# Two batches of a fused attention and feed-forward kernel: loads through one casting queue, and transposes moved from DMA to TensorE

## The chip, the cores and the metric

The kernel runs on one core of one Trainium2 chip. The metric is the device time of one execution in microseconds. The median of three runs before the change is 457.38 us.

## The reference

```python
def _attn_ref(q, k, v):                  # (8 batches, 12 heads, 448, 64) each
    S = q.shape[2]
    scale = 1.0 / np.sqrt(q.shape[-1])
    scores = scale * np.matmul(q, k.transpose(0, 1, 3, 2))
    attn = np.maximum(scores, 0.0) ** 2 / S
    return np.matmul(attn, v)

def _moe_ref(x, w_in, w_out):            # x (3584, 768), w_in (768, 2048), w_out (2048, 768)
    h = x @ w_in
    g = h * (1.0 / (1.0 + np.exp(-1.702 * h)))
    return g @ w_out
```

x is the attention's output with the heads side by side: row (batch, position), column (head, 64).

## The kernel before

**Units and slots.** The attention is cut into 24 units, three for each of 8 batches, with four heads each. The four heads are two pairs (s) of two (a). A unit's q, k and v lie with 128 partitions = (s, 64 positions) and, in each, 2 heads a by 7 x 64 values. A unit has seven slots j, one per seventh of its keys. A slot is `scores` (L124): four matmuls of 64x64 weights and 448 columns into a PSUM tile of the pool `ps_s`, which has two; `relu2` (L138): a relu on ScalarE (ACT), or on VectorE (DVE) in slot 3 of the first six units, and a square on VectorE; and `av_mm` (L149): the weighted sum, four matmuls, accumulated over the seven slots. `xt_evac` (L164) copies a finished unit into the activations `xt` of its group of tokens.

**Visits.** `visit(n)` (L184) issues the scores of the next n slots (two as a rule), then the weighted sums of the slots of the visit before, then the relus and squares of the new ones. All engines work in program order; nothing is reordered (L281).

**Products.** The tokens are cut into groups of 384 and 512 rows in turn. `m1(g, f)` (L204) is one of 16 column tiles of the first product: six matmuls on weights `win`, an activation on ScalarE and a scaling on GpSimd (POOL). `m2(g, m, h)` (L224) is the second product, 16 matmuls on `wout`. Both take PSUM from the pool `ps_m` (two buffers).

**How q and k come in.** `load_qk` (L73) loads f32 from SyncE's (SP's) queue. `cast` (L92) makes f16 on VectorE or GpSimd. `trans` (L103) turns it with DMA transposes, issued from SP, so that the 64 values of two heads lie on 128 partitions. Only unit 0 is turned by `trans_pe` (L111): seven transposes of 128 columns on TensorE (PE) into a tile of `ps_s`, copied out by ScalarE and VectorE. v is loaded and cast by one DMA on GpSimd's queue (L83), as are the weights: `w1(i)` (L246) brings a quarter of w_in in four DMAs, `w2(h, i)` (L253) a quarter of w_out in one. `sp_gate` (L259) and `pool_gate` (L262) hold a queue until something has landed.

**Order at the start (L281 to L339).** Units 0 to 2 are loaded from SP, v and the quarters of w_in come between from GpSimd, units 3 and 4 behind a gate. The slots of units 0 to 2 (batch 0) run alone (L299, L317). Then the 16 column tiles of the first group's first product alternate with the slots of units 3 to 5 (L322 to L337); in between, units 4 and 5 are cast and transposed and w_out is loaded. At L355 a gate waits for a quarter of w_out, the loads of units 6 and 7 are issued, and the first group's second product begins (L357). From there on products and visits alternate by a table of costs (L366 to L405), and each later unit is loaded and cast some units ahead.

The places that the prediction speaks of are the first score (L131), the first product proper (L212), the first second product (L230) and the first score of unit 6.

Of the kernel before, what the change touches and what calls it, by code (L numbers as in the profile page):

```python
# [15 lines left out]
def kernel(  # L16
# [9 lines left out]
    nc = tc.nc  # L26
# [19 lines left out]

    cst = ctx.enter_context(tc.tile_pool(name="cst", bufs=1))
    stp = ctx.enter_context(tc.tile_pool(name="stp", bufs=3))
    c16 = ctx.enter_context(tc.tile_pool(name="c16", bufs=2))
    v16p = ctx.enter_context(tc.tile_pool(name="v16p", bufs=5))  # L50
    qkT = ctx.enter_context(tc.tile_pool(name="qkT", bufs=3))
    rlp = ctx.enter_context(tc.tile_pool(name="rlp", bufs=3))
# [8 lines left out]

    ident = cst.tile([128, 128], F16, name="ident")
    gate = cst.tile([1, 64], F16, name="gate")
    gate2 = cst.tile([1, 1], F32, name="gate2")
    warm = cst.tile([1, 1], F32, name="warm")
    win = [cst.tile([128, 2, NP, WQ * 128], F16, name=f"win{i}") for i in range(NF // WQ)]
    wout = [[cst.tile([128, WO, NOUT], F16, name=f"wout{h}_{i}") for i in range(NF // WO)]
            for h in range(2)]


    units = {}

    def load_qk(u):  # L73
        b, pr = divmod(u, NP)
        st = units.setdefault(u, {})
        for n, t in (("k", k), ("q", q)):
            x = stp.tile([128, 2, S], F32, name=f"{n}st", tag=f"{n}st")
            nc.sync.dma_start(
                out=x,
                in_=t[b, 4 * pr:4 * pr + 4].rearrange("(a s) (p j) d -> (s p) a (j d)", a=2, j=J))  # L80
            st[n] = x

    def load_v(u):  # L83
        b, pr = divmod(u, NP)
        st = units.setdefault(u, {})
        x = v16p.tile([128, 2, S], F16, name="v16", tag="v16")
        nc.gpsimd.dma_start(  # L87
            out=x,
            in_=v[b, 4 * pr:4 * pr + 4].rearrange("(a s) (p j) d -> (s p) a (j d)", a=2, j=J))
        st["v16"] = x  # L90

    def cast(u, n, eng):  # L92
        st = units[u]
        c = c16.tile([128, J, 2, D], F16, name=f"{n}16", tag=f"{n}16")
        o = c.rearrange("p j a d -> p a j d")
        i = st[n].rearrange("p a (j d) -> p a j d", d=D)
        if eng is nc.scalar:
            eng.activation(out=o, in_=i, func=AF.Copy)
        else:
            eng.tensor_copy(out=o, in_=i)  # L100
        st[n + "16"] = c

    def trans(u):  # L103
        st = units[u]
        for n in ("k", "q"):
            t = qkT.tile([128, J, 128], F16, name=f"{n}T", tag=f"{n}T")
            nc.sync.dma_start_transpose(  # L107
                out=t[:, :, :], in_=st[n + "16"].rearrange("p j a d -> p (j a d)"))
            st[n + "T"] = t

    def trans_pe(u, n, cut):  # L111
        st = units[u]
        ps = ps_s.tile([128, 2, 1024], F16, name="tr", tag="sc")
        for j in range(J):
            nc.tensor.matmul(  # L115
                out=ps[:, 0, j * 128:(j + 1) * 128],
                lhsT=st[n + "16"][:, j, :, :], rhs=ident[:, :], is_transpose=True)
        t = qkT.tile([128, J, 128], F16, name=f"{n}T", tag=f"{n}T")
        nc.scalar.activation(out=t[:, 0:cut, :], in_=ps[:, 0, 0:cut * 128], func=AF.Copy)
        if cut < J:  # L120
# [17 lines left out]
    def relu2(u, j, sc):  # L138
        rl = rlp.tile([128, 2, S], F16, name="rl", tag="rl")
        at = atp.tile([128, 2, S], F16, name="at", tag="at")  # L140
        if u < 2 * NP and j == 3:
            nc.vector.tensor_scalar(out=rl, in0=sc[:, :, 0:S], scalar1=0.0, scalar2=None,  # L142
                                    op0=ALU.max)
        else:
            nc.scalar.activation(out=rl, in_=sc[:, :, 0:S], func=AF.Relu)  # L145
        nc.vector.tensor_tensor(out=at, in0=rl, in1=rl, op=ALU.mult)  # L146
        return at
# [16 lines left out]
    def xt_evac(u):  # L164
        b, pr = divmod(u, NP)
        av = units[u]["av"]
        lo = b * J
        while lo < (b + 1) * J:
            g = max(i for i in range(NG) if gcum[i] <= lo)
            hi = min((b + 1) * J, gcum[g + 1])  # L170
            if g not in xts:
                xts[g] = xtp.tile([128, 2, NP, 512], F16, name="xt", tag="xt")
            nc.vector.tensor_copy(  # L173
                out=xts[g][:, :, pr, 64 * (lo - gcum[g]):64 * (hi - gcum[g])],
                in_=av[:, :, 64 * (lo - b * J):64 * (hi - b * J)])
            lo = hi
        units[u] = None
# [26 lines left out]
    def m1(g, f):  # L204
        n = 64 * gblk[g]
        if f == 0:
            gts[g] = gtp.tile([128, NF, 512], F16, name="gt", tag="gt")
        ht = ps_m.tile([128, 512], F32, name="ht", tag="mm")
        w = win[f // WQ]
        fo = (f % WQ) * 128  # L210
        for kk in range(NK):
            nc.tensor.matmul(  # L212
                out=ht[:, 0:n], lhsT=w[:, kk // NP, kk % NP, fo:fo + 128],
                rhs=xts[g][:, kk // NP, kk % NP, 0:n],
                start=(kk == 0), stop=(kk == NK - 1))
        gf = gfp.tile([128, 512], F32, name="gf", tag="gf")
        nc.scalar.activation(out=gf[:, 0:n], in_=ht[:, 0:n],  # L217
                             func=AF.Gelu_apprx_sigmoid, scale=1.0 / SC)
        nc.gpsimd.tensor_scalar(out=gts[g][:, f, 0:n], in0=gf[:, 0:n],  # L219
                                scalar1=SC, scalar2=1.0, op0=ALU.mult, op1=ALU.mult)  # L220
# [20 lines left out]
                nc.sync.dma_start(out=out[r0:r0 + 63 * J + 1:J, :],  # L241
                                  in_=ot[64 * i:64 * i + 64, :])

    w_rows = moe_w_in.rearrange("(i a s d) f -> a d s i f", a=2, s=2, d=D)

    def w1(i):  # L246
        for a in range(2):
            for s in range(2):
                nc.gpsimd.dma_start(  # L249
                    out=win[i][64 * a:64 * a + 64, s, :, :],  # L250
                    in_=w_rows[a, :, s, :, i * WQ * 128:(i + 1) * WQ * 128])

    def w2(h, i):  # L253
        nc.gpsimd.dma_start(  # L254
# [26 lines left out]
    with tc.manual_schedule():  # L281
        nc.vector.memset(warm, 0.0)
        nc.scalar.activation(out=warm, in_=warm, func=AF.Gelu_apprx_sigmoid)
        make_identity(nc, ident)


        load_qk(0)
        load_qk(1)
        load_qk(2)
        load_v(0)  # L290
        cast(0, "k", nc.vector)
        trans_pe(0, "k", J)
        cast(0, "q", nc.vector)
        trans_pe(0, "q", 4)
        pool_gate(units[1]["k"][0:1, 0, 0:1])
        load_v(1)
        w1(0)
        cast(1, "k", nc.vector)
        visit(2)  # L299
        cast(1, "q", nc.vector)  # L300
        trans(1)
        cast(2, "k", nc.gpsimd)
        cast(2, "q", nc.gpsimd)
        trans(2)
        load_v(2)
        w1(1)
        sp_gate(win[0][64:65, 1, 0, 0:64])
        load_qk(3)
        load_v(3)
        w1(2)  # L310
        cast(3, "k", nc.gpsimd)
        cast(3, "q", nc.gpsimd)
        trans(3)
        load_qk(4)
        load_v(4)
        w1(3)
        while pos[0] < NP * J:  # L317
            visit(min(2, NP * J - pos[0]))
        visit(0)


        for f in range(NF):  # L322
            m1(0, f)
            if f >= 1 and (f % 4 != 3 or f == 15):
                visit(min(2, 2 * NP * J - pos[0]))
            if f == 2:
                cast(4, "k", nc.vector)
                cast(4, "q", nc.gpsimd)
                trans(4)
                load_qk(5)  # L330
                load_v(5)
            if f in (4, 5, 6, 7):
                w2((f - 4) // 2, f % 2)
            if f == 7:
                cast(5, "k", nc.vector)
                cast(5, "q", nc.gpsimd)
                trans(5)  # L337
# [98 lines left out]
```

## Time and profile before

| | us |
|---|---|
| median of 3 runs (455.9 to 1011.11) | 457.38 |
| the profiled execution | 456.6 |
| its span, first to last instruction | 454.8 |
| TensorE busy | 394.2 (87%) |
| ScalarE busy | 206.5 (45%) |
| VectorE busy | 193.9 (43%) |
| GpSimd busy | 132.4 (29%) |

Durations come from the profiled execution; its span is 1.8 us shorter than its time. Of the three runs one took 1011.11 us, the others 455.9 and 457.38. The profile names engines PE, PEld (weight loads of PE), DVE, ACT, POOL and SP; a matmul's duration runs from its start to its modelled end, so that overlapped matmuls add up to more than the time that they take together.

### The profile page before, as it was taken

How to read it: one execution, taken by the hardware profiler on the slowest of the kernel's cores; microseconds unless marked ns; L12 is line 12 of the kernel's file. 1: busy time of each engine (PE TensorE's matmuls, PEld its weight loads, DVE VectorE, ACT ScalarE, POOL GpSimd, SP SyncE). 2: the span in 40 equal slices, each digit the busy share in tenths (PEclk: the TensorE clock that was granted, in tenths of full speed). 3: DMA queues.
4: the chain of work that ended last, by engine and by line, in shares of the span. 5: the costliest groups of instructions: out<-in, count | busy, mean ns of one | idle time of the engine just before them, and what ended most of it. 6: DMA issues, size and time to landing. Idle time of an engine off the chain costs nothing.

```text
span 454.8 us, 7541 instructions
## 1 busy us (share of the span) xinstructions
PE 394.2 (87%) x3022; PEld 196.1 (43%) x3022; DVE 193.9 (43%) x292; ACT 206.5 (45%) x294; POOL 132.4 (29%) x203
## 2 busy tenths in 40 slices
PE   3255816299999999999999999999998999999995
PEld 1122303045443455544444555544444555555563
DVE  2555423343265565533644456455425643100121
ACT  4244424251577655536564555356555554222100
POOL 3714322213443422313323323313322311222200
PEclk9995767789999999999999999999999999999999
DMA  8999696954879772771853648745513311111132
GB/s 258 142 197 164 145 149 141 198 215 62 182 177 169 179 184 59 160 183 69 180 124 71 161 93 173 175 122 102 136 36 76 75 36 37 35 36 31 27 83 71
DMA packets 74340, 55.89 MB, mean 123 GB/s; under 512 B 45120, under 2 KB 70720, under 8 KB 74304
## 3 DMA queue, kind: packets, MB, share of 16 engines
q1 hardware_dynamic: 60288, 43.59, 39.5%
q0 software_dynamic: 14016, 11.80, 18.6%
q8 instruction: 24, 0.39, 0.4%
q14 instruction: 12, 0.10, 0.1%
HBM read 45.61 MB, written 11.01 MB: 124 GB/s over the span
## 4 chain that ended last, share of the span: by engine, by line
PE 74%; DMA 10%; DVE 5%; ACT 4%; issue 3%; POOL 2%; SPq 2%; ACTq 0%
PE op L230 31%; PE ht L212 30%; DMA qT<-q 8%; PE sc L131 7%; PE av L156 6%; ACT rl L145 3%; DVE xt L173 2%; DVE at L146 2%; DMA kst<-in_k_dram 2%; SPq L107 1%; DVE rl L142 1%; DVE k L100 1%; ACT gf L217 1%; POOL win L249 0%; DVE osb L235 0%
## 5 line engine op out<-in xcount | busy, mean ns | idle before, releaser
L145 ACT ACTIVATE rl<-sc 128x896 f16<-128x896 f32 x162 | 140.2, 918 | 92.2 <-PE sc L131 88.9
L212 PE MATMUL ht<-xt,win 128*128 128x384 f16 (+1 forms) x768 | 163.7, 359 | 4.4 <-DVE xt L173 4.4
L146 DVE TENSOR_TENSOR at<-rl 128x896 f16<-128x896 f16 x168 | 115.2, 703 | 113.1 <-ACT rl L145 112.9
L219 POOL TENSOR_SCALAR gt<-gf 128x384 f16<-128x384 f32 (+1 forms) x128 | 76.1, 595 | 270.1 <-ACT gf L217 268.8
L230 PE MATMUL op<-wout,gt 128*128 128x384 f16 x896 | 153.3, 326 | 0.0
L217 ACT ACTIVATE gf<-ht 128x384 f32<-128x384 f32 (+1 forms) x128 | 69.8, 545 | 123.3 <-PE ht L212 103.3
L230 PEld LDWEIGHTS <-gt 128*128 128x128 f16 x896 | 86.4, 98 | 62.9 <-issue 5.4
L212 PEld LDWEIGHTS <-win 128*128 128x128 f16 x768 | 71.4, 99 | 86.7 <-issue 29.8
L131 PE MATMUL sc<-qT,kT 64*64 64x448 f16 x672 | 55.9, 389 | 41.6 <-DMA qT<-q 32.4
L235 DVE TENSOR_SCALAR osb<-op 128x384 f32<-128x384 f32 x56 | 31.1, 556 | 114.8 <-PE op L230 114.8
L156 PE MATMUL av<-at,v 64*64 64x448 f16 x672 | 53.6, 379 | 4.0 <-DVE at L146 3.5
L131 PEld LDWEIGHTS <-kT 64*64 64x64 f16 x672 | 16.2, 109 | 76.2 <-issue 75.4
L173 DVE CAST xt<-av 128x768 f16<-128x768 f32 (+2 forms) x36 | 26.9, 774 | 21.7 <-PE av L156 21.4
L156 PEld LDWEIGHTS <-v 64*64 64x64 f16 x672 | 22.9, 112 | 21.5 <-issue 11.5
L100 POOL CAST q<-qst 128x896 f16<-128x896 f32 x22 | 21.1, 957 | 0.6 <-DMA qst<-in_q_dram 0.2
L87 POOL DMA_DIRECT2D v<-in_v_dram x24 | 18.4, 766 | 1.3 <-DMA win<-in_moe_w_in_dram 0.3
L100 DVE CAST k<-kst 128x896 f16<-128x896 f32 x22 | 16.7, 764 | 3.6 <-DMA kst<-in_k_dram 3.6
L249 POOL DMA_DIRECT2D win<-in_moe_w_in_dram x16 | 9.9, 625 | 3.7 <-DMA win<-in_moe_w_in_dram 3.1
L142 DVE TENSOR_SCALAR rl<-sc 128x896 f16<-128x896 f32 x6 | 6.5, 1079 | 0.0
L100 POOL CAST k<-kst 128x896 f16<-128x896 f32 x2 | 2.2, 1078 | 12.5 <-issue 12.5
L115 PE MATMUL tr<-ident,k 128*128 128x128 f16 x7 | 0.9, 310 | 5.0 <-DVE k L100 5.0
L254 POOL DMA_DIRECT2D wout<-in_moe_w_out_dram x4 | 3.7, 930 | 0.2
(17 smaller groups left out, 9.3 us busy)
## 6 DMA issues: line engine op xcount, KB each, us to landing
kst<-in_k_dram SPq DMA_DIRECT2D x24, 448.0 KB, 5.3
qst<-in_q_dram SPq DMA_DIRECT2D x24, 448.0 KB, 5.9
out_dram<-osb SPq DMA_DIRECT2D x56, 192.0 KB, 2.7
v<-in_v_dram POOLq DMA_DIRECT2D x24, 224.0 KB, 4.8
win<-in_moe_w_in_dram POOLq DMA_DIRECT2D x16, 192.0 KB, 9.7
wout<-in_moe_w_out_dram POOLq DMA_DIRECT2D x4, 768.0 KB, 10.2
kT<-k SPq DMA_TRANSPOSE x23, 3.0
qT<-q SPq DMA_TRANSPOSE x23, 3.0
```

What stands on the lines that cost most here:

```text
L87: nc.gpsimd.dma_start(out=x, in_=v[b, 4 * pr:4 * pr + 4].rearrange("(a s) (p j) d -> (s p) a (j d)", a=2, j=J))
L100: eng.tensor_copy(out=o, in_=i)
L131: nc.tensor.matmul(out=sc[c, a, 0:S], lhsT=st["kT"][r, j, c], rhs=st["qT"][r, :, c], start=True, stop=True)
L145: nc.scalar.activation(out=rl, in_=sc[:, :, 0:S], func=AF.Relu)
L146: nc.vector.tensor_tensor(out=at, in0=rl, in1=rl, op=ALU.mult)
L156: nc.tensor.matmul(out=st["av"][64 * a:64 * a + 64, s, 0:S], lhsT=st["v16"][r, a, 64 * j:64 * j + 64], rhs=at[r, a, :], start=(j == 0), st ...
L173: nc.vector.tensor_copy(out=xts[g][:, :, pr, 64 * (lo - gcum[g]):64 * (hi - gcum[g])], in_=av[:, :, 64 * (lo - b * J):64 * (hi - b * J)])
L212: nc.tensor.matmul(out=ht[:, 0:n], lhsT=w[:, kk // NP, kk % NP, fo:fo + 128], rhs=xts[g][:, kk // NP, kk % NP, 0:n], start=(kk == 0), stop ...
L217: nc.scalar.activation(out=gf[:, 0:n], in_=ht[:, 0:n], func=AF.Gelu_apprx_sigmoid, scale=1.0 / SC)
L219: nc.gpsimd.tensor_scalar(out=gts[g][:, f, 0:n], in0=gf[:, 0:n], scalar1=SC, scalar2=1.0, op0=ALU.mult, op1=ALU.mult)
L230: nc.tensor.matmul(out=op[:, 0:NOUT], lhsT=gts[g][:, f, m * 128:(m + 1) * 128], rhs=wout[h][f // WO][:, f % WO, :], start=(f == 0), stop=( ...
L235: nc.vector.tensor_scalar(out=ot[:, h * NOUT:(h + 1) * NOUT], in0=op[:, 0:NOUT], scalar1=1.0 / SC, scalar2=None, op0=ALU.mult)
```

## The change

For units 0 to 5 (batches 0 and 1) q and k no longer come as f32 over SP's queue. `load16` loads and casts them in one DMA on GpSimd's queue, where v and the weights already are, and the DMAs stand there in the order in which the data are used. TensorE transposes them: `trans_pe` now issues 14 transposes of 64 columns per tensor (one per slot and head a) instead of 7 of 128, because a loaded tile has its heads a outside of the slots j. It takes its PSUM from `ps_m` instead of `ps_s`, and with `cut` 0 the whole copy is VectorE's. Units are transposed a visit or more ahead, except 4 and 5, which are transposed just before the visit that first uses them. Later units are loaded and transposed as before.

The heads of a unit are chosen in another way (`quad`): heads a*6 + 2*pr + s instead of 4*pr + 2*a + s. With that a quarter of w_in comes in two DMAs of 64x6x512 instead of four of 64x3x512. The relu of slot 3 of units 0 to 2 moves from VectorE to ScalarE. The weights' last two quarters of w_in and the w_out quarters are issued after fixed column tiles of the first product (`pool_work`). `pool_gate` and the gate on w_in are gone. From L355 of the kernel before on, the program is the same.

```diff
-    c16 = ctx.enter_context(tc.tile_pool(name="c16", bufs=2))
+    c16 = ctx.enter_context(tc.tile_pool(name="c16", bufs=3))
...
-    win = [cst.tile([128, 2, NP, WQ * 128], F16, name=f"win{i}") for i in range(NF // WQ)]
+    win = [cst.tile([128, NK, WQ * 128], F16, name=f"win{i}") for i in range(NF // WQ)]
...
+    def quad(t, b, pr):
+        return t[b].rearrange("(a i s) (p j) d -> i (s p) a (j d)", a=2, i=NP, j=J)[pr]
...
+    def load16(u, n):
+        b, pr = divmod(u, NP)
+        st = units.setdefault(u, {})
+        x = c16.tile([128, 2, J, D], F16, name=f"{n}16", tag=f"{n}16")
+        nc.gpsimd.dma_start(
+            out=x,
+            in_=quad({"k": k, "q": q}[n], b, pr))
+        st[n + "16"] = x
+
     def trans_pe(u, n, cut):
+
         st = units[u]
-        ps = ps_s.tile([128, 2, 1024], F16, name="tr", tag="sc")
+        ps = ps_m.tile([128, 1024], F16, name="tr", tag="mm")
         for j in range(J):
-            nc.tensor.matmul(
-                out=ps[:, 0, j * 128:(j + 1) * 128],
-                lhsT=st[n + "16"][:, j, :, :], rhs=ident[:, :], is_transpose=True)
+            for a in range(2):
+                nc.tensor.matmul(
+                    out=ps[64 * a:64 * a + 64, j * 128:(j + 1) * 128],
+                    lhsT=st[n + "16"][:, a, j, :], rhs=ident[:, :], is_transpose=True)
         t = qkT.tile([128, J, 128], F16, name=f"{n}T", tag=f"{n}T")
-        nc.scalar.activation(out=t[:, 0:cut, :], in_=ps[:, 0, 0:cut * 128], func=AF.Copy)
+        if cut:
+            nc.scalar.activation(out=t[:, 0:cut, :], in_=ps[:, 0:cut * 128], func=AF.Copy)
         if cut < J:
-            nc.vector.tensor_copy(out=t[:, cut:J, :], in_=ps[:, 0, cut * 128:J * 128])
+            nc.vector.tensor_copy(out=t[:, cut:J, :], in_=ps[:, cut * 128:J * 128])
...
-        if u < 2 * NP and j == 3:
+        if NP <= u < 2 * NP and j == 3:
...
-    w_rows = moe_w_in.rearrange("(i a s d) f -> a d s i f", a=2, s=2, d=D)
+    w_rows = moe_w_in.rearrange("(a kk d) f -> a d kk f", a=2, d=D)
...
         for a in range(2):
-            for s in range(2):
-                nc.gpsimd.dma_start(
-                    out=win[i][64 * a:64 * a + 64, s, :, :],
-                    in_=w_rows[a, :, s, :, i * WQ * 128:(i + 1) * WQ * 128])
+            nc.gpsimd.dma_start(
+                out=win[i][64 * a:64 * a + 64, :, :],
+                in_=w_rows[a, :, :, i * WQ * 128:(i + 1) * WQ * 128])
...
+        load16(0, "k")
+        load16(0, "q")
         make_identity(nc, ident)
-
-
-        load_qk(0)
-        load_qk(1)
-        load_qk(2)
...
+        n = 0
         while pos[0] < NP * J:
             visit(min(2, NP * J - pos[0]))
+            n += 1
+            if n == 2:
+                trans_pe(1, "k", 0)
+                trans_pe(1, "q", 0)
+            if n == 5:
+                trans_pe(2, "k", 0)
+                trans_pe(2, "q", J)
+            if n == 9:
+                load16(4, "k")
+                load16(4, "q")
+            if n == 10:
+                trans_pe(3, "k", 0)
+                trans_pe(3, "q", 0)
         visit(0)
 
 
+        pool_work = {0: lambda: load_v(4), 1: lambda: w1(2),
+                     3: lambda: (load16(5, "k"), load16(5, "q")), 4: lambda: load_v(5),
+                     5: lambda: w1(3), 7: lambda: w2(0, 0), 8: lambda: w2(0, 1),
+                     9: lambda: w2(1, 0), 10: lambda: w2(1, 1)}
         for f in range(NF):
             m1(0, f)
-            if f >= 1 and (f % 4 != 3 or f == 15):
+            if f in (4, 9):
+                trans_pe(4 + f // 8, "k", 0)
+                trans_pe(4 + f // 8, "q", 0)
+            if f % 4 != 3:
                 visit(min(2, 2 * NP * J - pos[0]))
...
+            if f in pool_work:
+                pool_work[f]()
```

GpSimd's program before, from its first DMA; line numbers are those of the kernel before.

```order
L87 DMA v_129<-in_v_dram 128x2x448
L263 COPY gate_99<-kst 1x1
L87 DMA v_157<-in_v_dram 128x2x448
L249 DMA win_101<-in_moe_w_in_dram 64x3x512 x4
L100 CAST k_189<-kst 128x2x7x64
L100 CAST q_191<-qst 128x2x7x64
L87 DMA v_197<-in_v_dram 128x2x448
L249 DMA win_102<-in_moe_w_in_dram 64x3x512 x4
L87 DMA v_208<-in_v_dram 128x2x448
L249 DMA win_103<-in_moe_w_in_dram 64x3x512 x4
```

And now, from behind the identity (k and q of unit 0 stand ahead of it), in the lines of the changed kernel:

```order
L117 DMA k_120<-in_k_dram 128x2x448
L117 DMA q_122<-in_q_dram 128x2x448
L89 DMA v_124<-in_v_dram 128x2x448
L117 DMA k_126<-in_k_dram 128x2x448
L117 DMA q_128<-in_q_dram 128x2x448
L89 DMA v_130<-in_v_dram 128x2x448
L89 DMA v_132<-in_v_dram 128x2x448
L262 DMA win_100<-in_moe_w_in_dram 64x6x512 x2
L117 DMA k_136<-in_k_dram 128x2x448
L117 DMA q_138<-in_q_dram 128x2x448
L89 DMA v_140<-in_v_dram 128x2x448
L262 DMA win_101<-in_moe_w_in_dram 64x6x512 x2
```

The casts are gone from GpSimd, and the loads of q and k stand between those of v and the weights.

TensorE's program now, at the end of unit 4's transposes, in batch 1. q_484 is q of unit 4; of the scores that follow, four matmuls are unit 3's last slot and four unit 4's first:

```order
L128 LDWEIGHTS q_484
L128 MATMUL tr<-ident,q_484 64x128
L145 LDWEIGHTS kT
L145 MATMUL sc<-qT,kT 64x448
L145 LDWEIGHTS kT
L145 MATMUL sc<-qT,kT 64x448
```

The scores of a visit now follow the transposes of the unit that they begin. Before, TensorE had no transposes there, and SP issued two DMA transposes instead.

SP's program before, from its seventh DMA, with the gates on w_in (win) and w_out (wout):

```order
L107 DMA_TRANSPOSE kT<-k_163 128x7x128
L107 DMA_TRANSPOSE qT<-q_183 128x7x128
L107 DMA_TRANSPOSE kT<-k_189 128x7x128
L107 DMA_TRANSPOSE qT<-q_191 128x7x128
L260 DMA gate<-win_101 1x16x4
L78 DMA kst<-in_k_dram 128x2x448
```

And now, from its first DMA:

```order
L273 DMA gate<-wout_1_105 1x16x4
L80 DMA kst<-in_k_dram 128x2x448
L80 DMA qst<-in_q_dram 128x2x448
L80 DMA kst<-in_k_dram 128x2x448
L80 DMA qst<-in_q_dram 128x2x448
L80 DMA kst<-in_k_dram 128x2x448
L80 DMA qst<-in_q_dram 128x2x448
L109 DMA_TRANSPOSE kT<-k_1169 128x7x128
L109 DMA_TRANSPOSE qT<-q_1171 128x7x128
```

SP has nothing ahead of the gate on w_out any more, and its first DMA transposes are those of unit 6.

## Rows read from the trace of the kernel before

**Rows 1.** The page's busy shares, and TensorE's busy tenths in 40 slices.
```profile
PE 394.2 (87%) x3022; PEld 196.1 (43%) x3022; DVE 193.9 (43%) x292; ACT 206.5 (45%) x294; POOL 132.4 (29%) x203
...
PE   3255816299999999999999999999998999999995
```

**Rows 2.** Busy time by stretch: window, us, PE, PEld, DVE, ACT, POOL, PEclk, DMA, GB/s.
```profile
8.85:46.70 37.85, 18.59 (x168) 7.15 (x167) 20.63 (x30) 15.86 (x18) 17.67 (x25) 0.83 1.17 184
46.70:103.63 56.93, 33.55 (x268) 14.49 (x265) 21.89 (x30) 22.66 (x34) 14.76 (x22) 0.75 0.83 164
...
91.00:96.00 5.00, 5.00 (x32) 2.19 (x36) 2.16 (x3) 2.22 (x3) 0.51 (x1) 0.58 1.06 382
103.63:454.80 351.17, 340.18 (x2580) 173.02 (x2576) 149.73 (x228) 164.94 (x238) 98.36 (x149) 1.00 0.48 107
```

**Rows 3.** Waits over the span: who waited for whom, us, times, longest.
```profile
PE sc L131 <- DMA qT<-q: 32.4, 4, 12.5
```

**Rows 4.** Timeline of TensorE behind two waits: start, us, line, tiles, idle before.
```profile
71.72 0.59 PE L131 MATMUL sc<-qT,kT 64*64 64x448 f16 x4 [12.54 <-DMA qT<-q]
...
90.99 0.96 PE L131 MATMUL sc<-qT,kT 64*64 64x448 f16 x8 [7.73 <-DMA qT<-q]
...
92.63 3.35 PE L212 MATMUL ht<-xt,win 128*128 128x384 f16 x12
```

**Rows 5.** Timeline of the start, to the first relu.
```profile
5.00 0.67 PEld L115 LDWEIGHTS <-k 128*128 128x128 f16 x7 [5.00 <-DVE k L100]
5.01 0.93 PE L115 MATMUL tr<-ident,k 128*128 128x128 f16 x7 [5.01 <-DVE k L100]
...
7.81 0.60 ACT L119 ACTIVATE qT<-tr 128x512 f16<-128x512 f16 x1 [0.92 <-PE tr L115]
8.44 0.36 DVE L121 COPY qT<-tr 128x384 f16<-128x384 f16 x1 [1.65 <-ACT qT L119]
8.85 0.96 PE L131 MATMUL sc<-qT,kT 64*64 64x448 f16 x8 [1.08 <-DVE qT L121]
...
9.48 2.54 ACT L145 ACTIVATE rl<-sc 128x896 f16<-128x896 f32 x3 [1.08 <-PE sc L131]
```

**Rows 6.** Casting loads of v, issue to landing: the first, and one at 40 us.
```profile
DMA to landing us min/median/max: 8.1/8.1/8.1
...
DMA to landing us min/median/max: 4.9/4.9/4.9
```

**Rows 7.** DMA queues and issues from 60 to 70 us: the casting queue, a transpose.
```profile
q0 software_dynamic: 1808, 1.38, 89.7%
...
qT<-q SPq DMA_TRANSPOSE x1, 12.0
```

**Rows 8.** Costliest groups of the page: the relu on ScalarE.
```profile
L145 ACT ACTIVATE rl<-sc 128x896 f16<-128x896 f32 x162 | 140.2, 918 | 92.2 <-PE sc L131 88.9
```

**Rows 9.** Timeline at the end of batch 0: last relu, first product proper.
```profile
44.56 0.92 ACT L145 ACTIVATE rl<-sc 128x896 f16<-128x896 f32 x1 [0.20 <-PE sc L131]
...
47.83 3.22 PE L212 MATMUL ht<-xt,win 128*128 128x384 f16 x10 [0.30 <-DVE xt L173]
```

**Rows 10.** Timeline of TensorE at full clock: a pair of products, a pair of scores.
```profile
54.22 2.12 PE L212 MATMUL ht<-xt,win 128*128 128x384 f16 x12
...
95.91 0.57 PE L131 MATMUL sc<-qT,kT 64*64 64x448 f16 x8
```

**Rows 11.** Unit 6: its q's transpose, its first scores, and landings from 100 us.
```profile
114.17 1.24 SPq L107 DMA_TRANSPOSE qT<-q  x1
...
118.01 0.57 PE L131 MATMUL sc<-qT,kT 64*64 64x448 f16 x8
...
qT<-q SPq DMA_TRANSPOSE x3, 2.9
```

**Rows 12.** Timeline: weight issues on GpSimd beside VectorE's squares.
```profile
15.49 1.16 DVE L146 TENSOR_TENSOR at<-rl 128x896 f16<-128x896 f16 x2
...
15.93 1.85 POOL L249 DMA_DIRECT2D win<-in_moe_w_in_dram  x3
```

More of the change, by code (lines that the diff above doesn't have):

```diff
@@ L63 @@
     gate = cst.tile([1, 64], F16, name="gate")
-    gate2 = cst.tile([1, 1], F32, name="gate2")
     warm = cst.tile([1, 1], F32, name="warm")
-    win = [cst.tile([128, 2, NP, WQ * 128], F16, name=f"win{i}") for i in range(NF // WQ)]
+    win = [cst.tile([128, NK, WQ * 128], F16, name=f"win{i}") for i in range(NF // WQ)]
     wout = [[cst.tile([128, WO, NOUT], F16, name=f"wout{h}_{i}") for i in range(NF // WO)]
@@ L79, in load_qk @@
                 out=x,
-                in_=t[b, 4 * pr:4 * pr + 4].rearrange("(a s) (p j) d -> (s p) a (j d)", a=2, j=J))
+                in_=quad(t, b, pr))
             st[n] = x
@@ L88, in load_v @@
             out=x,
-            in_=v[b, 4 * pr:4 * pr + 4].rearrange("(a s) (p j) d -> (s p) a (j d)", a=2, j=J))
+            in_=quad(v, b, pr))
         st["v16"] = x
@@ L171, in xt_evac @@
             if g not in xts:
-                xts[g] = xtp.tile([128, 2, NP, 512], F16, name="xt", tag="xt")
+                xts[g] = xtp.tile([128, NK, 512], F16, name="xt", tag="xt")
             nc.vector.tensor_copy(
-                out=xts[g][:, :, pr, 64 * (lo - gcum[g]):64 * (hi - gcum[g])],
+                out=xts[g][:, 2 * pr:2 * pr + 2, 64 * (lo - gcum[g]):64 * (hi - gcum[g])],
                 in_=av[:, :, 64 * (lo - b * J):64 * (hi - b * J)])
@@ L212, in m1 @@
             nc.tensor.matmul(
-                out=ht[:, 0:n], lhsT=w[:, kk // NP, kk % NP, fo:fo + 128],
-                rhs=xts[g][:, kk // NP, kk % NP, 0:n],
+                out=ht[:, 0:n], lhsT=w[:, kk, fo:fo + 128],
+                rhs=xts[g][:, kk, 0:n],
                 start=(kk == 0), stop=(kk == NK - 1))
@@ L260, in sp_gate @@
         nc.sync.dma_start(out=gate[0:1, :], in_=src)
-    def pool_gate(src):
-        nc.gpsimd.tensor_copy(out=gate2[0:1, 0:1], in_=src)
     def t1(g):
@@ L283 @@
         nc.scalar.activation(out=warm, in_=warm, func=AF.Gelu_apprx_sigmoid)
+        load16(0, "k")
+        load16(0, "q")
         make_identity(nc, ident)
-        load_qk(0)
-        load_qk(1)
-        load_qk(2)
+        load16(1, "k")
+        load16(1, "q")
         load_v(0)
-        cast(0, "k", nc.vector)
+        load16(2, "k")
+        load16(2, "q")
+        load_v(1)
+        load_v(2)
+        w1(0)
+        for n in ("k", "q"):
+            load16(3, n)
+        load_v(3)
+        w1(1)
@@ L292 @@
         trans_pe(0, "k", J)
-        cast(0, "q", nc.vector)
         trans_pe(0, "q", 4)
[L295 to L316, printed above, removed]
+        n = 0
         while pos[0] < NP * J:
             visit(min(2, NP * J - pos[0]))
+            n += 1
[11 more added lines that the diff above has]
+                trans_pe(3, "q", 0)
@@ L325 @@
                 visit(min(2, 2 * NP * J - pos[0]))
[L326 to L337, printed above, removed]
+            if f in pool_work:
+                pool_work[f]()
```

## The prediction

> **What bounds the kernel now.** I read the page's busy shares and slices first [rows 1]: TensorE is busy 87% of the span, and nearly all that it is not busy lies in the first nine slices of 11.4 us. The table by stretch says it sharper [rows 2]: from 103.63 us, where the first group's second product starts, to the end TensorE is busy 340.18 of 351.17 us. Before that it is busy 18.59 of 37.85 us while batch 0's attention runs (8.85 to 46.70) and 33.55 of 56.93 us while batch 1's attention is woven into the first group's first product (46.70 to 103.63). So the change can win only ahead of 103.63, and what it wins there moves all the rest forward, because the rest is TensorE-bound.
>
> Next the waits: scores wait for a transposed q four times, 32.4 us in all, the longest 12.5 [rows 3]. TensorE's timeline has two of them, 12.54 us before 71.72 and 7.73 before 90.99 [rows 4]. The DMA transposes of small packets stand there behind casting weight loads. The other two lie in batch 0. These waits are what the change removes: q and k of units 0 to 5 arrive in f16, and TensorE transposes them.
>
> I cut the sum into four stages. A runs to the first score, B to the first product proper (47.83), C to 103.63, D is the rest.
>
> **A, to the first score: no change, from -2 to +3.4.** Now k is loaded, cast and transposed, and the first score starts at 8.85 [rows 5]. After, the cast falls away, but k and q come over the casting queue. A casting load of the same size took 4.9 us from issue to landing in mid-kernel and 8.1 as the first of all [rows 6]. The first was then sharing the engines with six plain loads, which are gone. With 4.9, k lands about 5.5 us after the start, q one transfer later. A transfer of 0.229 MB takes 1.5 us at what this queue moved when it was backed up, 1.38 MB at a share of 89.7% of 10 us, 0.154 MB/us [rows 7]. q at 7.0 plus the transposes (0.93), ACT's copy of four columns (0.60) and VectorE's of three (0.36) [rows 5] is 8.9. With 8.1 it is 12.1; if nothing but the transfer counts it is under 7.
>
> **B, batch 0's attention: -10.1.** Now 38.98 us (8.85 to 47.83). After, ACT sets the pace, since its relu of batch 0's 21 slots all stand on it (three were VectorE's):
> - 0.63 from the first score to the first relu [rows 5];
> - 21 x 0.918 = 19.28 [rows 8], and ACT's copy of unit 2's q, 0.60 x 896/512 = 1.05;
> - three insertions of a unit's transposes in TensorE's order, each two tensors;
> - 2.35 from the end of the last relu (45.48) to the product (47.83) [rows 9], as now.
>
> A tensor was seven transposes of 128 columns, 0.93 us [rows 5]. It is now fourteen of 64 columns. The trace shows none. If the two column halves run side by side, it is 0.93 again. If weight loads go one after another at 0.67/7 = 0.096 [rows 5], it is 14 x 0.096 + 0.31 = 1.65. If nothing is pipelined, at the 0.31 of one matmul (the row's x7 with only the starts apart is the nearest), 4.34. I take 0.93, since the 64-wide scores of four quarters do run side by side (eight matmuls of 448 columns in 0.57 [rows 10]). An insertion costs 1.86, three 5.6. VectorE's copies of k and q lie beside the next scores, which belong to the unit before, and cost nothing while that holds.
> Sum 0.63 + 19.28 + 1.05 + 5.6 + 2.35 = 28.9. Saved 38.98 - 28.9 = 10.1; the product starts at 37.7.
>
> Data are there in time by the 1.5 us per tensor and 5.1 per weight quarter (0.786 MB). From a first landing at 5.5, unit 1's q is in at 10, unit 2's at 14.5, w1(0) at 22, unit 3's q at 25, w1(1) at 32. Unit 1 is transposed after two visits (about 13), unit 3 after ten (about 33).
>
> **C, batch 1 with the first product: -17.5.** Now 55.80 us (47.83 to 103.63). Off go the waits, 12.54 + 7.73 = 20.27. What they leave also goes: the stretch after each runs at the lower clock. After 90.99 eight scores took 0.96 and twelve product matmuls 3.35; at full clock 0.57 and 2.12 [rows 4, 10]. That is 0.39 + 1.23, and about 0.4 for the weighted sums, 2.0; after the first wait, with one product instead of two, 1.2. Together 3.2.
> Added are two insertions (units 4 and 5). Here the scores of the new unit stand in the very next visit, so TensorE waits for VectorE's copy of q as well: 0.36 x 896/384 = 0.84, and a little for what stands before it on VectorE; I take 1.1. Behind this wait stand the weighted sums and the next product on TensorE, so it is paid in full. 2 x (1.86 + 1.1) = 5.9.
> The two casts of k on VectorE and of q on GpSimd that fall away were hidden and count nothing. 55.80 - 20.27 - 3.2 + 5.9 = 38.2; the second product starts at 76.0.
>
> The weights keep pace, barely. GpSimd issues the second-layer quarters after products 7 to 10 of 16, so from about 37.7 + 8/16 x 38.2 = 57. Four quarters take 20.5, so the two that are needed at 76 land at 67, the last two at 78, and those are used only behind five or more products of the next group.
>
> **D, after: +2, from 0 to +8.** Unit 6 still comes over plain loads and DMA transposes. Now its q's transpose is issued at 114.17 and its scores start at 118.01; such a transpose landed in 2.9 us [rows 11]. That leaves 0.9 us. Before, no weight load was left by then. After, the gate on SP opens at about 67, and behind it six plain loads of 1.2 us each (0.459 MB at the 382 GB/s of 91 to 96 [rows 2]), the last two weight quarters and three casting loads of v share the engines: 67 + 7.2 + 10.3 + 4.5 = 89. The transpose, 10.5 us into D, starts at 86.5, still in this traffic. A transpose in such traffic took 12.0 [rows 7], which would cost 8; the overlap is about 3 us, so I take 2.
>
> **Sum.** -10.1 - 17.5 + 2 = -25.6 on the profiled span of 454.8, 429.2; with the 1.8 us around it (456.6 against 454.8) 431.0 us. The profiled execution is 0.8 us under the median of 457.38.
>
> **Rivals.**
> 1. *The insertions are cheaper.* Transposes at full clock and beside ACT's relu cost half, and D costs nothing: 5 insertions x 0.9 + 2 = 6.5 less, 424.5. For it: ACT and not TensorE sets the pace in B. Against: ACT cannot run ahead, as scores have two buffers.
> 2. *The one casting queue runs late.* Everything for two batches and all weights is now behind one another: 18 tensors x 1.5 + 8 quarters x 5.1 = 68 us, and the first half of w_out must be in by 76. The spare is 9 to 19 us. If each of some 30 issues loses 0.6 us, the spare is gone and the product slips by up to 10 us: 436 to 444. For it: the last weights fit with little to spare. Against: three weight issues in a row, beside two squares on VectorE, took 1.85, 0.62 each [rows 12], less than a tensor's 1.5.
> The Trainium skill (SBUF — State Buffer, "SBUF: two separate sides") warns of this: descriptors of loads issued from GpSimd can't be written while VectorE holds the port they share. [...]
> 3. *The clock stays low.* If the transposes leave TensorE at the lower of its two levels through C, sixteen products cost 0.62 more each (1.23/2) and eleven visits 0.8: 9.9 + 8.8 = 18.7, 450: no change by the measure. Against: TensorE would be busy about 80% of C, as it is where the clock is full now.
> The Trainium skill (TensorE: Matmul & The Clock Gate, "Part 4: PE-mode transpose") says transposes don't count as work that raises the clock. No run here shows that; by it this rival is likelier.
> 4. *The 64-column transposes don't pipeline: slower.* 12 tensors x 14 x 0.31 = 52 us, against 12 x 0.93 = 11: +41, 472. It makes the kernel slower than before from about 0.23 us a transpose, (26 + 11)/168. For it: halving the columns doubles the instructions. Against: the 128-column ones went at 0.10 apart.
>
> **Chances.** The forecast (426 to 436) 0.50; rival 1 (419 to 426) 0.22; rival 2 (436 to 446) 0.20; rival 3 0.06; rival 4 0.02. The range leaves out the far ends of 1 and 2, and 3 and 4: 421 to 444. A difference under 2% can't be told from none by this measurement, so faster means under 448.2: 0.50 + 0.22 + 0.20 and a little of rival 3, 0.93; within 2% 0.05; slower 0.02.
>
> **What would show it.** The wait for a transposed q should be gone before the second product, which should start near 76; the first product near 38; seven-column tensors should take about 1 us of TensorE; TensorE should pause about 1.1 us before units 4 and 5; the first scores of unit 6 may wait for a DMA transpose, some 2 us. I am wrong if the second product starts after 90, if products there wait for a weight load, or if the part after it grows beyond 355 us.

## The result, and the profile after

The changed kernel takes 423.61 us (median of four runs, 423.12 to 424.21). Against the kernel before the ratio is 0.927, interval 0.925 to 0.930: 7.3% faster. The forecast was 431.0 with a range of 421 to 444: the time lies in the range, but below the band of 426 to 436 that stood for the forecast itself.

The table by stretch of the changed kernel, cut at the same events as in the prediction: first score, first product proper, start of the second product, end. Columns as in [rows 2].

```profile
8.28:32.82 24.54, 18.42 (x257) 9.09 (x256) 18.63 (x32) 18.40 (x22) 6.38 (x10) 1.00 0.99 159
32.82:66.13 33.31, 29.88 (x316) 14.53 (x316) 21.54 (x32) 21.79 (x33) 17.69 (x27) 1.00 1.01 148
66.13:422.30 356.17, 342.19 (x2578) 173.30 (x2575) 149.10 (x228) 165.65 (x239) 98.25 (x149) 0.99 0.52 115
```

Beside the forecast, in us:

| stage | before | forecast | after | after - forecast |
|---|---|---|---|---|
| A, to the first score | 8.85 | 8.85 | 8.28 | -0.6 |
| B, batch 0, to the product proper | 38.98 | 28.9 | 24.54 | -4.4 |
| C, batch 1 with the first product | 55.80 | 38.2 | 33.31 | -4.9 |
| D, from the second product on | 351.17 | 353.2 | 356.17 | +3.0 |

So the 32.5 us of the profiled spans (454.8 to 422.3) are 37.5 won ahead of the second product and 5.0 given back behind it.

The waits of the changed kernel's TensorE. The row that answers to [rows 3] is the first:

```profile
PE sc L145 <- DMA qT<-q: 4.4, 1, 4.4
...
PE sc L145 <- DVE qT L135: 2.2, 3, 1.1
```

The four waits for a DMA-transposed q in batches 0 and 1, 32.4 us, are gone, and one of 4.4 is new. Of the waits for VectorE's copies, 2.2 us in three places, 1.08 is unit 0's and stood there before [rows 5]; the two at units 4 and 5 are new, 1.16 together, where the forecast had 1.1 each. The one wait of scores for a DMA is at unit 6, the first unit that is still transposed by DMA. In the timeline, TensorE there, and the SP issues ahead of it:

```profile
76.08 1.33 SPq L109 DMA_TRANSPOSE kT<-k  x1
...
77.52 5.07 SPq L109 DMA_TRANSPOSE qT<-q  x1
...
84.97 0.96 PE L145 MATMUL sc<-qT,kT 64*64 64x448 f16 x8 [4.41 <-DMA qT<-q]
...
85.87 2.74 PE L226 MATMUL ht<-xt,win 128*128 128x512 f16 x6
...
92.81 0.57 PE L145 MATMUL sc<-qT,kT 64*64 64x448 f16 x8
```

The pause costs more than itself. Behind it the granted clock is 0.50, the lower of TensorE's two levels (1.2 and 2.4 GHz), and eight scores take 0.96 there and six product matmuls of 512 columns 2.74:

```profile
84.97:89.40 4.43, 4.42 (x26) 1.41 (x30) 1.25 (x2) 2.41 (x4) 0.00 (x0) 0.50 1.19 286
```

In the kernel before, where no pause stood ahead of them, unit 6's scores took 0.57 and the product behind them 1.47:

```profile
118.52 1.47 PE L212 MATMUL ht<-xt,win 128*128 128x512 f16 x6
...
124.12 0.57 PE L131 MATMUL sc<-qT,kT 64*64 64x448 f16 x8
```

From unit 6's first scores to the scores at 92.81 and 124.12, the same place in both programs, it is 7.84 us now and was 6.11 [rows 11], so the lower level costs 1.7 us on top of the 4.4.

### The profile page after: what moved, and what is told of

Read it like the earlier page. It is cut to its first block, busy times and chain, and to the rows that moved or that the text cites. A ratio compares the mean times of both kernels' runs of the same rounds, so it can differ in the third digit from the quotient of the medians.

```text
span 422.3 us, 7800 instructions
## 1 busy us (share of the span) xinstructions
PE 392.4 (93%) x3176; PEld 198.5 (47%) x3176; DVE 189.7 (45%) x292; ACT 208.8 (49%) x298; POOL 129.5 (31%) x200
## 4 chain that ended last, share of the span: by engine, by line
PE 78%; DVE 8%; ACT 6%; issue 3%; DMA 3%; POOL 1%; ACTq 0%; POOLq 0%
PE op L244 34%; PE ht L226 31%; PE sc L145 7%; PE av L170 6%; ACT rl L159 5%; DVE at L160 3%; DVE xt L187 2%; DMA qT<-q 2%; DMA q<-in_q_dram 1%; PE tr L128 1%; ACT gf L231 1%; DVE k L102 1%; DVE qT L135 0%; POOL gt L233 0%; DVE osb L249 0%
## 5 line engine op out<-in xcount | busy, mean ns | idle before, releaser
L226 PE MATMUL ht<-xt,win 128*128 128x384 f16 (+1 forms) x768 | 161.4, 355 | 2.5 <-DVE xt L187 2.5
L160 DVE TENSOR_TENSOR at<-rl 128x896 f16<-128x896 f16 x168 | 111.8, 679 | 93.3 <-ACT rl L159 93.1
L145 PE MATMUL sc<-qT,kT 64*64 64x448 f16 x672 | 53.0, 375 | 12.2 <-ACT rl L159 5.1
L170 PE MATMUL av<-at,v 64*64 64x448 f16 x672 | 50.9, 359 | 4.2 <-DVE at L160 3.2
L187 DVE CAST xt<-av 128x768 f16<-128x768 f32 (+2 forms) x36 | 26.9, 774 | 7.5 <-PE av L170 7.3
L102 POOL CAST q<-qst 128x896 f16<-128x896 f32 x18 | 16.9, 939 | 5.1 <-DMA qst<-in_q_dram 4.9
L128 PE MATMUL tr<-ident,k 128*64 128x128 f16 x84 | 4.2, 253 | 5.2 <-DMA k<-in_k_dram 5.2
L128 PEld LDWEIGHTS <-k 128*64 128x64 f16 x84 | 3.1, 129 | 6.8 <-DMA k<-in_k_dram 5.2
L135 DVE COPY qT<-tr 128x896 f16<-128x896 f16 (+1 forms) x5 | 2.8, 568 | 7.2 <-ACT qT L133 7.0
L262 POOL DMA_DIRECT2D win<-in_moe_w_in_dram x8 | 5.5, 692 | 1.0 <-DMA v<-in_v_dram 0.5
L117 POOL DMA_DIRECT2D k<-in_k_dram x6 | 4.6, 764 | 1.8 <-DMA v<-in_v_dram 0.9
```

Of the source, the lines that this page charges most:

```text
L145: nc.tensor.matmul(out=sc[c, a, 0:S], lhsT=st["kT"][r, j, c], rhs=st["qT"][r, :, c], start=True, stop=True)
L170: nc.tensor.matmul(out=st["av"][64 * a:64 * a + 64, s, 0:S], lhsT=st["v16"][r, a, 64 * j:64 * j + 64], rhs=at[r, a, :], start=(j == 0), st ...
L187: nc.vector.tensor_copy(out=xts[g][:, 2 * pr:2 * pr + 2, 64 * (lo - gcum[g]):64 * (hi - gcum[g])], in_=av[:, :, 64 * (lo - b * J):64 * (hi ...
L226: nc.tensor.matmul(out=ht[:, 0:n], lhsT=w[:, kk, fo:fo + 128], rhs=xts[g][:, kk, 0:n], start=(kk == 0), stop=(kk == NK - 1))
```

## The experiments

Each run stands beside the kernel before on the same chip, 452.9 to 456.3 us there, and the ratios are to that. The transposes alone, the layout, the transposes twice and the earlier transfers ran on one chip, where the changed kernel was not run (kernel before 452.86). The others ran on another chip with the changed kernel beside them, 425.28 us (ratio 0.932, 0.929 to 0.936; kernel before 456.29) and 424.15 us (0.932, 0.928 to 0.936; 455.31).

The theory: the gain is the waits for DMA transposes, and what is given back is such a wait at unit 6. The rivals: the order of the loads on the casting queue is what counts, or the layout.

**Transposes alone.** The kernel before, with the transposes of units 1 to 5 on TensorE and nothing else.

```diff
-        trans(1)
...
+            if n == 2:
+                trans_pe(1, "k", 0)
+                trans_pe(1, "q", 0)
```

(likewise units 2 to 5, with c16 of four buffers and `trans_pe` of seven 128-column transposes in `ps_m`)

> The kernel before, with only the DMA transposes of units 1 to 5 replaced by seven 128-column transposes per tensor on TensorE (in ps_m, copied out as in the change, placed at the same visits); plain loads, casts, queues, gates and weight DMAs stay. Theory (the DMA transposes behind the weight loads were the wait; loads and casts were in time): the wait of scores for a q falls from 32.4 us to under 5, the second product starts at about 75, the time is 425 to 435. Rival (the order of the loads on one casting queue is needed as well, since units 3 to 5 are loaded behind gates and weights): the waits move to the casts, TensorE idles as long before units 3, 4 or 5, and the time is 440 to 455.

Measured: 425.93 us, ratio 0.941 (0.936 to 0.946); second product at 72.78. No wait for a DMA transpose is left at all. Its stretches (the middle cut, 36.00, lies 1.2 us ahead of the first product proper, 37.23):

```profile
8.79:36.00 27.21, 20.18 (x210) 9.09 (x209) 22.56 (x35) 16.46 (x19) 18.00 (x25) 0.90 1.09 233
36.00:72.78 36.78, 32.27 (x297) 15.38 (x293) 24.31 (x34) 22.57 (x34) 15.16 (x22) 0.94 1.02 203
72.78:424.10 351.32, 340.17 (x2580) 173.01 (x2576) 149.86 (x228) 164.97 (x238) 98.68 (x149) 1.00 0.51 107
```

The theory holds and the rival falls: this one part alone gives a ratio of 0.941, where the whole change gives 0.927 to 0.932. The last row needs 351.32 us, as in the kernel before (351.17), and not 356.17: with the plain loads unit 6 does not wait. Of what the other parts win ahead of the second product (72.78 to 66.13, 6.6 us), 4.9 are given back behind it.

**Transposes and the relu's place.** The same, with slot 3's relu of units 0 to 2 on ScalarE.

```diff
-        if u < 2 * NP and j == 3:
+        if NP <= u < 2 * NP and j == 3:
```

> The kernel before with its plain loads, casts and gates, with two parts of the change: the transposes of units 1 to 5 on TensorE (128 columns) and the relu of slot 3 of units 0 to 2 on ScalarE. With the transposes alone the second product started at 72.78, 6.6 us behind the changed kernel; moving that relu back in the changed kernel cost 3.0 there. Theory (transposes and relu carry the gain; the casting queue's part ahead of the second product is some 3.5 us and is given back at unit 6, where the plain loads leave no wait): second product at 69 to 71, no wait of unit 6, time within 2 us of the changed kernel beside it. Rival (the casting queue is worth what it saves ahead of the second product): second product at 69 to 71, but the time 3 us or more above the changed kernel's.

Measured: 426.09 us (0.937, 0.933 to 0.940), the changed kernel beside it 424.15; the second product at 71.25, a little later than expected, and no wait of unit 6. The time is 1.9 us above the changed kernel's, as the theory has it, and the intervals of the two ratios overlap. So what the casting queue is worth in the end (with the layout and the narrower transposes, which come with it) is not told apart from nothing, though the second product starts 4.5 us later here than in the changed kernel beside it (66.77). Part of what the plain loads cost ahead of it shows in one row: TensorE waits 2.01 us for the q of unit 3, which GpSimd casts.

```profile
31.64 0.93 PE L115 MATMUL tr<-ident,q 128*128 128x128 f16 x7 [2.01 <-POOL q L100]
```

**The relu's place alone, undone.** The changed kernel with that relu back on VectorE.

```diff
-        if NP <= u < 2 * NP and j == 3:
+        if u < 2 * NP and j == 3:
```

> The changed kernel with the relu of slot 3 of units 0 to 2 back on VectorE (as in the kernel before). Theory (ScalarE paces batch 0 at 0.81 us a relu): three relus fewer there, batch 0 shorter by 1 to 2.4 us, time lower by as much. Rival (VectorE is as full as ScalarE, 7.04 of 8 us busy from 16 to 24, and its relu of 1.08 us stands ahead of the squares): batch 0 longer by 1 to 2 us, time higher by as much.

Measured: 427.2 us (0.937, 0.933 to 0.940), the changed kernel beside it 425.28; second product at 69.15 against 66.18. The theory fell: the second product is later, by 3.0 us, which is more than the rival's 1 to 2. The time is 1.9 us higher, but the intervals of the two ratios overlap, so the direction is shown ahead of the second product only. ScalarE's pauses show why. In the changed kernel its relus stand in rows of six and seven; here they break up and wait for scores, and scores wait for VectorE's relu:

```profile
23.62 2.54 ACT L159 ACTIVATE rl<-sc 128x896 f16<-128x896 f32 x3 [0.20 <-PE sc L145]
27.67 0.92 ACT L159 ACTIVATE rl<-sc 128x896 f16<-128x896 f32 x1 [1.51 <-PE sc L145]
29.01 0.92 ACT L159 ACTIVATE rl<-sc 128x896 f16<-128x896 f32 x1 [0.42 <-DVE at L160]
31.92 0.92 ACT L159 ACTIVATE rl<-sc 128x896 f16<-128x896 f32 x1 [1.99 <-PE sc L145]
```
```profile
21.81 0.38 PE L145 MATMUL sc<-qT,kT 64*64 64x448 f16 x4 [0.68 <-DVE rl L156]
...
28.38 0.59 PE L145 MATMUL sc<-qT,kT 64*64 64x448 f16 x4 [0.75 <-DVE rl L156]
```

TensorE also runs lower behind these pauses. Its granted clock from 26 to 37 us is 0.55 here (first row) and 1.00 in the changed kernel beside it (second), and how much of the 3.0 us is the clock's no run separates.

```profile
26.00:37.00 11.00, 8.85 (x83) 3.97 (x83) 7.14 (x12) 3.66 (x6) 0.20 (x1) 0.55 0.24 39
26.00:37.00 11.00, 8.48 (x107) 4.01 (x108) 7.38 (x14) 6.86 (x9) 2.20 (x4) 1.00 0.31 45
```

So the relu's move belongs to what the change wins ahead of the second product.

**The layout alone.** The kernel before with the other choice of heads: w_in in two DMAs per quarter, `win` and `xt` to fit.

```diff
-    w_rows = moe_w_in.rearrange("(i a s d) f -> a d s i f", a=2, s=2, d=D)
+    w_rows = moe_w_in.rearrange("(a kk d) f -> a d kk f", a=2, d=D)
```

> The kernel before, with only the other choice of heads: two DMAs of 64x6x512 per quarter of w_in instead of four of 64x3x512, and the tiles win and xt laid out to fit. Theory (it only makes the weight DMAs fewer): 455 to 458, no change. Rival (half as many issues on GpSimd let the loads behind them start sooner, and so part of the gain is the layout's): 448 or less.

Measured: ratio 0.990, interval 0.979 to 1.001, and single runs from 445.43 to 455.99. That is not told apart from no change, and a gain of up to 2% is not excluded; below the rival's 448 was one execution of four. In that one, which is the profiled one, four waits for a transposed q add up to 26.9 us, where [rows 3] had 32.4. So the layout leaves these waits there; the run with the transposes alone, in the old layout, has none of them.

**Transposes twice.** The changed kernel with each transpose issued twice.

```diff
-        for j in range(J):
+        for j in [x % J for x in range(2 * J)]:
             for a in range(2):
```

> The changed kernel with each of the 14 transposes of a tensor issued twice (the second writes the same values again). It prices a transpose where it stands. Twelve tensors at 0.56 to 0.58 us at full clock and 0.96 at the lower are 8 to 9 us more on TensorE. Theory (in batch 0 ScalarE sets the pace and hides most of a transpose after the first insertion; in batch 1 it is paid): +4 to +6 us, 428 to 430. Rival (transposes are paid in full wherever they stand): +8 to +9 us, 432 to 433. Second rival (all hidden): within 1 us of 423.6.

Measured: 430.11 us (0.951, 0.944 to 0.957); second product at 70.71, 4.6 us behind the change's 66.13. The times don't decide between the theory and the rival: 430.11 is 6.5 us above the 423.61, but the ratios lie further apart (0.951 against 0.927 to 0.932), and the changed kernel was not run on that chip. The traces decide. A tensor with fourteen more transposes takes 0.97 instead of 0.58 at full clock, 0.39 more. The stretches B and C, cut at the same events as in the table of the changed kernel:

```profile
9.30:36.55 27.25, 20.00 (x341) 11.93 (x341) 18.95 (x32) 18.45 (x22) 5.36 (x8) 0.87 0.85 138
36.55:70.71 34.16, 31.05 (x372) 15.88 (x372) 21.73 (x32) 21.79 (x33) 17.74 (x27) 1.00 0.99 146
```

The first score is 1.0 us later, batch 0 is 2.7 longer and C 0.9. By the durations in the timelines the doubled transposes take 2.8 us more in batch 0 and 1.5 in C. So the theory's total came, but not its split: batch 0 hid nothing (its granted clock is also lower, 0.87 against 1.00), and C hid about half. The start of this run says something about the clock, below.

**Earlier transfers.** The changed kernel with the casting DMAs of batch 1 and of the weights issued earlier.

```diff
             if n == 9:
                 load16(4, "k")
                 load16(4, "q")
+                load_v(4)
+                w1(2)
...
-        pool_work = {0: lambda: load_v(4), 1: lambda: w1(2),
-                     3: lambda: (load16(5, "k"), load16(5, "q")), 4: lambda: load_v(5),
-                     5: lambda: w1(3), 7: lambda: w2(0, 0), 8: lambda: w2(0, 1),
-                     9: lambda: w2(1, 0), 10: lambda: w2(1, 1)}
+        pool_work = {0: lambda: (load16(5, "k"), load16(5, "q")), 1: lambda: load_v(5),
+                     2: lambda: w1(3), 4: lambda: w2(0, 0), 5: lambda: w2(0, 1),
+                     6: lambda: w2(1, 0), 7: lambda: w2(1, 1)}
```

> The changed kernel with the casting DMAs of batch 1 and of the weights issued earlier, nothing else: v of unit 4 and the third quarter of w_in already at visit 9 of batch 0 (the DMA engines are half idle from 24 to 40 us), and the rest three places earlier in GpSimd's program. Theory (unit 6's scores wait 4.4 us because its DMA transposes share the engines with the last casting loads): the wait goes under 1 us, TensorE keeps its clock there, and the time falls by 4 to 6 us, to 418 to 420. Rival (the wait comes from SP and GpSimd issuing late, or the traffic only moves and catches the plain loads of unit 6): within 2 us of 423.6.

Measured: 418.66 us, ratio 0.926 (0.920 to 0.932) against a kernel before of 452.86 on that chip. This ratio is not told apart from the changed kernel's, which was not run there; the run of both parts, below, has it beside it. What the trace shows is clear: unit 6's wait is gone, and D is 349.96 long instead of 356.17. First the DMA view of the changed kernel from 76 to 86 us, in 40 slices, with the casting queue's share and the transposes' time from issue to landing:

```profile
DMA  9999999999999999999996253200999999979999
...
q0 software_dynamic: 654, 0.54, 37.0%
...
kT<-k SPq DMA_TRANSPOSE x2, 6.4
qT<-q SPq DMA_TRANSPOSE x2, 5.8
```

and the same ten microseconds with the earlier transfers:

```profile
DMA  0000007999639999299994000089995926698999
...
q0 software_dynamic: 1, 0.00, 0.1%
...
kT<-k SPq DMA_TRANSPOSE x2, 3.0
qT<-q SPq DMA_TRANSPOSE x2, 3.0
```

In the first the engines are full until 81.5 us and the casting queue has 37% of their time; in the second it is done, and a transpose lands in 3.0 us, where the kernel before had 2.9 [rows 11]. SyncE begins to issue q's transpose at nearly the same time in both (77.52 and 77.68), but the issue itself takes 5.07 us in the first (above) and 1.22 here:

```profile
77.68 1.22 SPq L109 DMA_TRANSPOSE qT<-q  x1
```

This shows what the wait was: not a late issue, but other transfers in the same engines. Which ones, the run does not separate, for it moves two kinds. The gate on w_out, too, opens earlier:

```profile
56.79 0.61 SPq L273 DMA_DIRECT2D gate<-wout  x1
```

In the changed kernel that is at 64.33, and the plain loads behind it are issued from 65.01 on and take 12.5 us (the median for q) to land, so they too are still under way when the transposes are issued:

```profile
64.33 0.62 SPq L273 DMA_DIRECT2D gate<-wout  x1
...
qst<-in_q_dram SPq DMA_DIRECT2D x3, 448.0 KB, 12.5
```

**Earlier transposes.** The changed kernel with units 4 and 5 transposed one column tile earlier.

```diff
-            if f in (4, 9):
+            if f in (3, 8):
```

> The changed kernel with units 4 and 5 transposed one column tile of the first product earlier (behind f = 3 and 8 instead of 4 and 9), so that VectorE's copies have a product or a visit beside them. Theory (TensorE's wait for the copy, 0.40 and 0.76 us in the changed kernel, is paid in full): 1 to 1.5 us less, second product at about 65. Rival (VectorE and ScalarE, not TensorE, set the pace there, and the wait is taken up by the next one): within 0.5 us of the base. In either case unit 6 still waits.

Measured: 426.56 us (0.935, 0.932 to 0.939) beside 425.28. That is neither the theory's gain nor a difference that the intervals show. The second product starts at 65.34 instead of 66.18, so the wait for the copies was paid, and 0.84 is won there. And it is lost again at once:

```profile
65.34 7.96 PE L244 MATMUL op<-wout,gt 128*128 128x384 f16 x48
...
75.97 6.80 SPq L109 DMA_TRANSPOSE qT<-q  x1
...
86.49 0.96 PE L145 MATMUL sc<-qT,kT 64*64 64x448 f16 x8 [6.71 <-DMA qT<-q]
```

Beside it, the changed kernel on the same chip:

```profile
66.18 7.96 PE L244 MATMUL op<-wout,gt 128*128 128x384 f16 x48
...
76.82 6.11 SPq L109 DMA_TRANSPOSE qT<-q  x1
...
85.97 0.96 PE L145 MATMUL sc<-qT,kT 64*64 64x448 f16 x8 [5.35 <-DMA qT<-q]
```

Unit 6's scores start at nearly the same time in both, whatever TensorE did before. The issue of q's transpose on SyncE, too, begins at different times and ends at nearly the same, 82.77 here and 82.93 beside it. There the transfers, not TensorE, set the time.

**Both earlier.**

> Earlier transfers (the casting DMAs of batch 1 and the weights three places earlier) and earlier transposes (units 4 and 5 one column tile earlier) together. If the two gains add: 417 to 418, below the 418.7 of the earlier transfers alone and 5 to 7 us below the base. If the second is taken up elsewhere: 418 to 419.5.

Measured: 417.52 us (0.916, 0.913 to 0.919), 7.8 us below the changed kernel beside it, with the intervals well apart. D is 349.98. So the earlier transfers do pay. Whether the earlier transposes add to them is not shown: the second product starts at 66.42 against 67.04 with the transfers alone, but that is one profiled execution each, on two chips. This is the fastest kernel of the study.

## Why the prediction was right

**The mechanism held.** TensorE idled ahead of the second product, and waits for DMA transposes were most of it. The run with the transposes alone shows that: one part, no change in the loads, and the waits are gone. That other transfers made these transposes late is read from the kernel before (12.0 us to land beside a casting queue at 89.7% [rows 7], 2.9 without [rows 11]); an experiment shows it for unit 6 only.

**The number is in part luck.** The stages missed by -0.6, -4.4, -4.9 and +3.0 us; that the last has the other sign brings the total nearer. With D as forecast the profiled execution would have taken 421.0, the very edge of the range. The time lies in rival 1's band (419 to 426), to which the prediction gave 0.22, and not in its own.

**A was right.** 8.28 where I had kept 8.85. k landed at 5.2, within 0.3 of the 5.5 that the mid-kernel load gave. That fits the view that the 8.1 of the first load [rows 6] came from the six plain loads beside it, but no run separates it.

**B was 4.4 too long, mainly by two terms.** The first is "21 x 0.918 = 19.28". A relu takes 0.92, but ScalarE starts the next before it is over:

```profile
14.24 4.96 ACT L159 ACTIVATE rl<-sc 128x896 f16<-128x896 f32 x6 [1.98 <-PE sc L145]
19.15 0.92 ACT L133 ACTIVATE qT<-tr 128x896 f16<-128x896 f16 x1
19.96 5.77 ACT L159 ACTIVATE rl<-sc 128x896 f16<-128x896 f32 x7
```

Six in 4.96 with a last one of 0.92 are 0.81 apart, so 21 are 17.0, 2.3 less. [rows 5] had said so: three in 2.54, again 0.81. The second is the three insertions at 1.86. ScalarE's pauses at them are 1.98, none and 0.44, some 2.4 in all against 5.6, 3.2 less. The first came at the lower clock (0.96 a tensor), and it was paid in full. The others came at full clock (0.58 and 0.56), and at the second ScalarE had the copy of q between its relus and enough ahead of it. Two more pauses of ScalarE, 0.49 and 0.20, and the longer last relu of each row, some 0.6, go the other way.

**C was 4.9 too long.** At full clock a tensor is 0.58, not 0.93:

```profile
41.64 0.58 PE L128 MATMUL tr<-ident,k 128*64 128x128 f16 x14
...
42.35 0.58 PE L128 MATMUL tr<-ident,q 128*64 128x128 f16 x14
...
43.64 0.38 PE L145 MATMUL sc<-qT,kT 64*64 64x448 f16 x4 [0.40 <-DVE qT L135]
...
54.87 0.57 PE L145 MATMUL sc<-qT,kT 64*64 64x448 f16 x8 [0.76 <-DVE qT L135]
```

Four tensors make 1.4 less. The waits for the copies are 0.40 and 0.76 instead of 1.1 each, 1.0 together. The first products, 3.22 us for ten matmuls at the lower clock in [rows 9], run at full clock, some 1.5 less. I had left that out. The remaining 1 us I can't place; the casts that left VectorE and GpSimd, which I counted at nothing, may hold it, but no run shows that.

**D was 3.0 too short.** The place and the cause were right, the size was not. The forecast had q's transpose issued at 86.5 and the traffic end at 89, some 3 us of overlap. It was issued at 77.52 and the traffic ended at 81.5, 4.0 us later: the second product came 9.9 us ahead of the forecast, the end of the transfers only 7.5. This is what the earlier-transposes run repeats on a small scale. And the lower clock behind the wait, 1.7 us, had been put at nothing. Without the wait D is 349.96 (the earlier transfers), so wait and clock cost 6.2 us, where the forecast had 2 on top of 351.17. Why D without the wait is 1.2 us shorter than in the kernel before stays open. The prediction's own sign, "if the part after it grows beyond 355 us", came true by 1.2 us: this step was mis-sized, though the direction and the total held.

**The rivals.** Rival 1's 424.5 is the nearest time, for half of its reasons: the insertions did cost about half, but D did not cost nothing. Rival 2 came true, if at all, behind the second product only, at unit 6; no product waited for a weight. The Trainium skill (SBUF — State Buffer, "SBUF: two separate sides") has it that GpSimd can't write the descriptors of its loads while VectorE runs an instruction in a two-port mode. No longer issue shows here: the load of k at 3.40, when VectorE had nothing to do, took 0.72, that of q at 17.86, beside a square and a copy out of PSUM, 0.71. Whether these two instructions, or the squares of [rows 12], run in such a mode no run here shows, so this is no test of that rule.

```profile
3.40 0.72 POOL L117 DMA_DIRECT2D k<-in_k_dram  x1
...
17.86 0.71 POOL L117 DMA_DIRECT2D q<-in_q_dram  x1 [0.97 <-DMA win<-in_moe_w_in_dram]
```

Rival 3 fell: the granted clock is 1.00 in C, and its twelve product matmuls take 2.12 as at full clock before [rows 10]. Rival 4 fell at the first row: fourteen half-width transposes take 0.96 where seven full ones take 0.93 at the lower clock, and 0.58 against 0.56 at full clock in the run with 128 columns. (Its break-even, (26 + 11)/168, is 0.22, not 0.23; nothing hangs on it.)

## What to carry to other kernels

A wait on a DMA of small packets behind bulk transfers can be removed by doing that step on an engine, even where this costs the busiest engine time: here ten tensors at 0.56 to 0.96 us of TensorE took away waits of 32.4 us. When work ahead of a transfer-bound point is shortened, look at the next thing that the transfers deliver: here part of the gain was lost there until the transfers themselves started earlier. Price a run of equal instructions by the distance of their starts, not by the duration of one.

## What the runs showed of the hardware that was not expected

Transposes alone brought TensorE to its higher level. In the run with each transpose issued twice, TensorE did nothing but 56 transposes from 5.16 us on, and the first scores behind them took 0.57 for eight, their time at the higher level [rows 10]:

```profile
5.16 1.70 PE L128 MATMUL tr<-ident,k 128*64 128x128 f16 x28 [5.16 <-DMA k<-in_k_dram]
...
6.74 1.48 PE L128 MATMUL tr<-ident,q 128*64 128x128 f16 x28
...
9.30 0.57 PE L145 MATMUL sc<-qT,kT 64*64 64x448 f16 x8 [1.08 <-DVE qT L135]
...
11.51 0.59 PE L145 MATMUL sc<-qT,kT 64*64 64x448 f16 x4 [0.42 <-ACT rl L159]
```

In the changed kernel, with half as many, they took 0.96 at 8.28. The level was lost again soon: four scores at 11.51 took 0.59, their time at the lower level. (The table's clock is no help at the start: it is 1.00 in both kernels up to the first scores, and in the changed kernel also where they took 0.96.) It is one profiled execution. The Trainium skill (TensorE: Matmul & The Clock Gate, "Part 4: PE-mode transpose") has it that transposes don't raise the clock; this run doesn't agree.

Half-width transposes go two for one: a 64-column transpose added 0.39/14 = 0.028 us at full clock, and fourteen of them took 0.58 where seven of 128 columns took 0.56, so twice the instructions cost next to nothing.
